# Decode attention over two layers: the last batch's second-layer loads as single parts, four under way

## The chip, the core and the metric

The kernel runs on one core of a Trainium2 chip. The core has a matrix engine (TensorE, rows PE for its matmuls and PEld for its weight loads), VectorE (DVE), ScalarE (ACT), GpSimd (POOL), SyncE (SP, which here only issues transfers), and 16 DMA engines that carry data between HBM and on-chip memory. The metric is the device time of one execution in microseconds (us), lower is better. Times of runs without a profile are given as a median of several; a profiled execution is a single one with its own time.

## The reference

Eight sequences, one new token each, go through two layers with the same weights and the same caches. A layer is attention over a cache of 4096 positions, then a small feed-forward part:

```
x = x + A(layernorm(x))      # attention: 16 query heads, 8 heads of K and V, 256 wide
x = x + B(layernorm(x))      # feed-forward part
x = x + A(layernorm(x))
x = x + B(layernorm(x))
# A: scores = q k^T / 16 ; p = softmax(scores) ; o = p v ; o wo
```

The caches `k_cache` and `v_cache` have the shape (8 batches, 8 heads, 4096 positions, 256) in bfloat16. That is 134 MB each, read from HBM; all else is small. Q has one row per sequence and head, so the work is moving the caches.

## The kernel before, in words

**Units and parts.** The work is a list `units` of 144 entries: (layer, batch, head), or a gap between layers. The second layer of a batch starts while the first layer of the next batch runs. The last section, from index `max(fence)` = 136 on, is the second layer of batch 7, with its heads in the order 2, 3, 6, 7, 4, 5, 0, 1; beside it nothing else is left to do. A head's K and V are each cut into four parts of 512 KB, and a part is moved into one of 31 slots of the tile `slab` (`N_SLOTS`, 4 KB for each of 128 partitions).

**What is done with a part.** A K part is transposed by VectorE into another slot (L605, two instructions). The scores are 16 matmuls for each part (L721, `k_part`). After the four parts of a head come maxima and exponentials (L736 and L755 on VectorE, L745, L773 and L783 on TensorE, L758 and L791 on ScalarE). The V parts follow one head later, 16 matmuls each (L698, `v_part`), and after the fourth `head_out` scales the result (L650). `mark` multiplies with wo (L185). In the first layer, transposed K of six heads and a few parts more stay on the chip for the second layer. So the last section loads 32 parts of V but only 7 of K, for the heads 0 and 1. After the last head comes a last feed-forward part for all batches (L954 to L1035), and the output is stored (L1036).

**The order of loads.** A planner makes the list `loads` before any instruction is written: K parts by the due times `by`, V parts by `plan`. Entries of kind "p" are no transfers: they bring a part that was parked in PSUM back into a slot. `pump()` takes from this list while more than one slot is free (`RESERVE`). It is called whenever a slot is given back: after a V part's matmuls, after the scores of a K part that is needed no more, and after a transpose. All loads go to SP's one queue, in this order, and each waits there until its slot has been read for the last time.

**Pairs.** Where two parts (2j, 2j+1) of the same head are both near in the list and two neighbouring slots are free, `pump` loads both with one transfer of 1 MB. Where no two neighbouring slots are free and at least seven parts are under way, it may put off the load instead (L556). In the last section the trace has 27 loads: 15 of one part (4 of K for head 0, one of K for head 1, 10 of V) and 12 of two (one of K, 11 of V), from 1034.74 to 1076.13 us. A ninth load is held until the one eight before it has landed: the issues at 1047.29 and 1048.53 follow such landings by 0.06 us.

```
            if i % 2 == 0 and two in wide and two in loads[-PAIR_VIEW:]:
                x = take_two() if len(free) > RESERVE + 1 else []
```

Of the kernel before, what the change touches and what calls it, by code (L numbers as in the profile page):

```python
# [25 lines left out]
PAIR_VIEW = 12  # L26
SETTLE = 3
BEFORE = 1


@with_exitstack
def kernel(
# [14 lines left out]
    nc = tc.nc  # L47
# [332 lines left out]
    fence = {}  # L380
# [28 lines left out]
    def fresh(u, s):  # L409

        return u is not GAP and (u[0] == 1 or not stays(u[1], u[2], s))
# [4 lines left out]
    t = 0  # L416
    while t < n_units:
# [5 lines left out]
        n = 1  # L423
# [14 lines left out]
    parts = [(t, s) for t in range(n_units) for s in range(4) if fresh(units[t], s)]  # L438
# [16 lines left out]
    for t in order:  # L455
        for s in range(4):
            i = late_v.get((t, s), 4 * t + s + LAG)
            if t in ends or units[t + 1 : t + 2] == [GAP]:
                i = 4 * t + (6, 6, 7, 7)[s]
            elif t + 2 == n_units:  # L460
                i = 4 * t + (7, 8, 8, 8)[s]
            elif t + 1 == n_units:
                i = 4 * t + (5, 5, 6, 6)[s]
# [3 lines left out]
    loads = []  # L467
    wide = set()
    calm = [any(f < t for f in [-1] + list(fence) if not any(f < e < t for e in ends)) for t in range(n_units + 2)]
    firm = set()  # L470
    at_ease = [all(calm[max(t - SETTLE, 0) : t + BEFORE]) for t in range(n_units + 1)]
    k = 0
    for i in range(4 * n_units + 8):
        n = len(loads)
# [8 lines left out]
        for far in (2, 12):  # L483
            t, q = divmod(i + far, 4)
# [8 lines left out]
    def take():  # L493

        lone = [x for x in free if x ^ 1 not in free]
        x = min(lone or free)
        free.remove(x)
        return x

    def take_two():  # L500

        both = [x for x in free if x % 2 == 0 and x + 1 in free]
        if both:
            free.remove(both[0])
            free.remove(both[0] + 1)
        return both[:1]
# [12 lines left out]
        )  # L519
    extra.append((w4_sb[:], B_w4.rearrange("(c p) d -> p c d", p=128)))  # L520
    n_loads = [0]

    at_out, at_exp, at_max = [], ([], []), ([], [])

    def bring(x, pieces, now):

        dst = slots[x].rearrange("p (e q c x) -> p q c e x", e=4, q=2, c=4)

        def move(q, lo, hi, home):
            src = home.bitcast(BF16).rearrange("p (c e x) -> p c e x", c=4, e=hi - lo)  # L530
            nc.scalar.copy(dst[:, q, :, lo:hi], src)  # L531

        for n, p in enumerate(pieces):
            if now:
                move(*p)
            else:
                (at_out if n < 2 else at_exp[n - 2]).append(lambda p=p: move(*p))

    def pump():
        while loads and len(free) > RESERVE:  # L540
            kind, t, i = loads[-1]
            _, b, g = units[t]
            if kind == "p":
                loads.pop()
                x = take()
                bring(x, park[parked[g, i]], g not in loose)
                kt_of[(1, b, g), i] = x
                continue
            cache, of = (A_k_cache, raw_of) if kind == "k" else (A_v_cache, v_of)
            n, two = 1, (kind, t, i + 1)  # L550
            if i % 2 == 0 and two in wide and two in loads[-PAIR_VIEW:]:
                x = take_two() if len(free) > RESERVE + 1 else []
                if x:
                    n, x = 2, x[0]
                    loads.remove(two)
                elif under_way[0] >= ENOUGH and two in firm:  # L556
                    return
            loads.pop()
            if n == 1:
                x = take()  # L560
            src = cache[b, g].rearrange("(p s e) d -> p s (e d)", s=4, e=8)
            nc.sync.dma_start(
                slab[:, UNIT * x : UNIT * (x + n)].rearrange("p (s d) -> p s d", s=n),
                src[:, i : i + n],
            )
            for m in range(n):
                of[t, i + m] = x + m
            under_way[0] += n
            n_loads[0] += n
            if n_loads[0] >= 8 and extra:  # L570
                nc.sync.dma_start(*extra.pop(0))
# [3 lines left out]
    def let_go(raw):  # L575

        free.append(raw)
        under_way[0] -= 1
        pump()
# [104 lines left out]
    def v_part(t, s):  # L684
        if s == 0:
            n = n_v[0]
            n_v[0] += 1
            at = PO + 4 * (n % n_po)
            pos[t] = pyb[:, at : at + 4].rearrange("p (k h) -> p k h", h=2)
            if n > n_po // 2 and n % (n_po // 2) == n_po // 4:  # L690
                clear.append(PO + 2 * n_po * (1 - n // (n_po // 2) % 2))
            if n % (n_po // 2) == n_po // 2 - 1:
                zero()
        v = v_of.pop((t, s))
        vv = slots[v].rearrange("p (c d) -> p c d", d=Dh)
        for c in range(8):
            for k in range(2):
                nc.tensor.matmul(  # L698
                    pos[t][:, k, :],
                    vv[:, c, k:Dh:2],  # L700
                    pts[t][:, 8 * s + c, :],
                    start=(n_v[0] == 1 and s == 0 and c == 0 and k == 0),
                    stop=True,
                    skip_group_check=True,
                )
        free.append(v)
        under_way[0] -= 1
        pump()

    def k_part(t, s):  # L710
        u = units[t]
        p, b, g = u
        if s == 0:
            assert t not in runs or t in ready
            scs[t] = scb[t % 2][:, 0:64].rearrange("p (c b h) -> p c b h", b=4, h=2)
        key = (u if fresh(u, s) else (1, b, g)), s
        ktv = slots[kt_of[key]].rearrange("p (e c m x) -> p e c m x", e=4, c=2, x=2)
        for c in range(2):
            for db in range(4):
                for x in range(2):  # L720
                    nc.tensor.matmul(  # L721
                        scs[t][:, 2 * s + c, :, :],
                        ktv[:, db, c, :, x],
                        Qblk[run_of[t][0]][:, run_of[t][1], db, x, :, :],
                        start=(db == 0 and x == 0),
                        stop=(db == 3 and x == 1),
                    )
        if p == 2 or not stays(b, g, s) or (g, s) in parked:
            free.append(kt_of.pop(key))
            pump()  # L730
# [154 lines left out]
    for t in range(n_units + 1):  # L885
        cur = t < n_units
        for q in range(4):
            i = 4 * t + q
# [178 lines left out]
```

## Time and profile before

| | |
|---|---|
| median of 3 runs | 1104.24 us (1102.91 to 1107.24) |
| profiled execution | 1111.46 us, span 1109.6 us |
| read from HBM | 443.1 MB, 399 GB/s over the span |
| DMA share, 1041 to 1090 us | 0.98, at 403 GB/s |
| PE busy, 1041 to 1090 us | 34.35 of 49 us |
| DMA share, 1090 to 1110 us | 0.01 |
| landing of the last load of the caches | 1090.54 us |

The page of the profile gives the busy time of each engine, its share in 40 slices of the span, the DMA queues, the chain of waits that ended last, and the costliest groups of instructions. In a group, "out<-in" are the program's names, "x" is the count, and the time in brackets is idle time of the engine and what ended it. "issue" as the end of idle time means that nothing the profile shows ended it. A transfer is listed at SP (SPq) when it is issued; its landing is the update of its semaphore. q1 is the queue of the kernel's transfers; q8 and q14 carry instructions.

### The profile page before, as it was taken

How to read it: one execution, taken by the hardware profiler on the slowest of the kernel's cores; microseconds unless marked ns; L12 is line 12 of the kernel's file. 1: busy time of each engine (PE TensorE's matmuls, PEld its weight loads, DVE VectorE, ACT ScalarE, POOL GpSimd, SP SyncE). 2: the span in 40 equal slices, each digit the busy share in tenths (PEclk: the TensorE clock that was granted, in tenths of full speed). 3: DMA queues.
4: the chain of work that ended last, by engine and by line, in shares of the span. 5: the costliest groups of instructions: out<-in, count | busy, mean ns of one | idle time of the engine just before them, and what ended most of it. 6: DMA issues, size and time to landing. Idle time of an engine off the chain costs nothing.

```text
span 1109.6 us, 46438 instructions
## 1 busy us (share of the span) xinstructions
PE 692.4 (62%) x20757; PEld 647.4 (58%) x20757; DVE 552.8 (50%) x1340; ACT 322.8 (29%) x1409; POOL 104.2 (9%) x156
## 2 busy tenths in 40 slices
PE   3345666667666766657656565766666566666766
PEld 2334666556556655656556565666656565566665
DVE  4447556642664346642566336743466425654222
ACT  1112135221342224221342214321243213421242
POOL 0001011100111001110011001110011100110011
DMA  9999999999999999999999999999999999999992
GB/s 365 403 419 424 402 418 413 426 400 416 420 415 404 404 417 424 425 415 404 419 387 423 405 407 414 405 404 398 417 425 423 405 394 380 413 401 414 416 419 99
DMA packets 92311, 446.10 MB, mean 402 GB/s; under 512 B 9920, under 2 KB 13904, under 8 KB 63440
## 3 DMA queue, kind: packets, MB, share of 16 engines
q1 hardware_dynamic: 92112, 443.14, 98.3%
q8 instruction: 162, 2.65, 0.9%
q14 instruction: 37, 0.30, 0.1%
HBM read 443.10 MB, written 0.01 MB: 399 GB/s over the span
## 4 chain that ended last, share of the span: by engine, by line
DMA 54%; PE 18%; DVE 10%; ACT 10%; issue 6%; SPq 1%; DVEq 0%; ACTq 0%; POOL 0%
DMA slab<-in_A_v_cache_dram 41%; DMA slab<-in_A_k_cache_dram 13%; PE bank L698 6%; DVE slab L605 6%; PE bank L721 4%; ACT pt L791 3%; ACT slab L531 2%; ACT pe L758 2%; DVE small L755 2%; PE bank L745 2%; PE bank L783 1%; ACT pt_far L791 1%; PE bank L773 1%; PE bank L141 1%; PE bank L185 1%
## 5 line engine op out<-in xcount | busy, mean ns | idle before, releaser
L605 DVE STREAM_TRANSPOSE slab<-slab 128x512 f32<-128x512 f32 x626 | 405.1, 686 | 192.0 <-DMA slab<-in_A_k_cache_dram 158.0
L698 PEld LDWEIGHTS <-slab 128*128 128x128 bf16 x8192 | 271.9, 105 | 245.3 <-DMA slab<-in_A_v_cache_dram 180.9
L721 PE MATMUL bank<-Qblk,slab 128*128 128x8 bf16 x8192 | 297.0, 168 | 73.8 <-DVE slab L605 33.8
L698 PE MATMUL bank<-pt,slab 128*128 128x2 bf16 x6336 | 230.7, 166 | 175.1 <-DMA slab<-in_A_v_cache_dram 118.0
L721 PEld LDWEIGHTS <-slab 128*128 128x128 bf16 x8192 | 269.1, 105 | 83.7 <-issue 41.9
L758 ACT ACTIVATE pe<-bank,small 128x32 bf16<-128x32 f32 x256 | 61.4, 297 | 365.9 <-DVE small L755 365.9
L802 POOL TENSOR_TENSOR small<-small 128x2 f32<-128x2 f32 x99 | 69.2, 699 | 706.2 <-DVE small L798 706.2
L755 DVE TENSOR_REDUCE small<-bank 128x2 f32<-128x256 f32 x128 | 54.2, 423 | 101.2 <-PE bank L745 101.1
L791 ACT CAST pt<-bank 32x64 bf16<-32x64 f32 x396 | 80.5, 203 | 81.3 <-PE bank L783 77.8
L698 PE MATMUL bank<-pt_far,slab 128*128 128x2 bf16 x1856 | 65.9, 166 | 42.1 <-DMA slab<-in_A_v_cache_dram 34.1
L798 DVE TENSOR_REDUCE small<-bank 128x2 f32<-128x64 f32 x128 | 27.5, 215 | 111.7 <-ACT pt L791 88.4
L170 ACT CAST Qblk<-bank 32x32 bf16<-32x32 f32 (+1 forms) x292 | 51.5, 176 | 98.5 <-PE bank L164 95.8
L745 PE MATMUL bank<-rows,small 128*128 128x128 bf16 x256 | 48.5, 293 | 30.3 <-DVE small L736 23.4
L783 PEld LDWEIGHTS <-rows 128*128 128x128 bf16 x512 | 33.6, 123 | 47.0 <-issue 46.7
L773 PE MATMUL bank<-pe,small 128*128 128x64 bf16 x128 | 27.2, 213 | 51.8 <-ACT pe L758 46.9
L650 ACT ACTIVATE qT<-bank,small 128x2 bf16<-128x2 f32 x198 | 41.8, 266 | 48.8 <-PE bank L698 46.7
L783 PE MATMUL bank<-pe,rows 128*128 128x64 bf16 x512 | 51.1, 240 | 4.3 <-issue 4.3
L736 DVE TENSOR_REDUCE small<-bank 128x2 bf16<-128x64 f32 x128 | 26.2, 204 | 49.5 <-PE bank L721 48.8
L185 PE MATMUL bank<-qT,wo_sb 128*128 128x1 bf16 (+1 forms) x1152 | 38.7, 165 | 6.7 <-ACT qT L650 5.0
L185 PEld LDWEIGHTS <-wo_sb 128*128 128x128 bf16 x1152 | 35.9, 104 | 7.5 <-issue 6.7
L745 PEld LDWEIGHTS <-small 128*128 128x128 bf16 x256 | 17.4, 106 | 32.6 <-DVE small L736 29.5
L650 ACT ACTIVATE qT<-bank,rz_far 128x2 bf16<-128x2 f32 x58 | 12.2, 265 | 81.8 <-PE bank L698 81.6
(118 smaller groups left out, 448.5 us busy)
## 6 DMA issues: line engine op xcount, KB each, us to landing
slab<-in_A_v_cache_dram SPq DMA_DIRECT2D x270, 512.0 KB, 8.6
slab<-in_A_v_cache_dram SPq DMA_DIRECT2D x121, 1024.0 KB, 12.3
slab<-in_A_k_cache_dram SPq DMA_DIRECT2D x100, 1024.0 KB, 12.0
slab<-in_A_k_cache_dram SPq DMA_DIRECT2D x113, 512.0 KB, 9.3
wo_sb<-in_A_wo_dram SPq DMA_DIRECT2D x4, 896.0 KB, 15.0
wq_sb<-in_A_wq_dram SPq DMA_DIRECT2D x3, 1024.0 KB, 6.8
w_sb<-in_B_w_dram SPq DMA_DIRECT2D x1, 1568.0 KB
w_sb<-in_B_w_dram SPq DMA_DIRECT2D x3, 448.0 KB, 17.0
```

The lines of the kernel that those rows point to most:

```text
L170: nc.scalar.copy(dst, src)
L185: nc.tensor.matmul(y[:, c, :], chunk(wo_sb[:, k, :], c), o[:, k, :], start=first and k == 4 * g and c == 0, stop=True, skip_group_check=True,)
L605: nc.vector.transpose(dst[:, q], src[:, q])
L650: nc.scalar.mul(qT1[:, k : k + 2, b], pos[t][:, :, h], rz_of[t][:, h : h + 1])
L698: nc.tensor.matmul(pos[t][:, k, :], vv[:, c, k:Dh:2], pts[t][:, 8 * s + c, :], start=(n_v[0] == 1 and s == 0 and c == 0 and k == 0), stop= ...
L721: nc.tensor.matmul(scs[t][:, 2 * s + c, :, :], ktv[:, db, c, :, x], Qblk[run_of[t][0]][:, run_of[t][1], db, x, :, :], start=(db == 0 and x ...
L745: nc.tensor.matmul(mzs[t][:, 128 * h : 128 * h + 128], pm[:, h : h + 1].to_broadcast([128, 128]), ident, start=True, stop=True,)
L755: nc.vector.tensor_reduce(nm, mx, AX.X, ALU.max, negate=True)
L758: nc.scalar.activation(pe[:].rearrange("p c b h -> p h (c b)")[:, h], scs[t].rearrange("p c b h -> p h (c b)")[:, h], ACT.Exp, bias=nm[:, ...
L783: nc.tensor.matmul(pp[:, c], sel, pe[:], start=True, stop=True)
L791: nc.scalar.copy(pts[t][sl].rearrange("p (k c) h -> p k c h", c=4), pp[sl, :, :, pb, :].rearrange("p c k h -> p k c h"),)
L802: nc.gpsimd.tensor_tensor(out=rz_of[t], in0=zs, in1=mone, op=ALU.pow)
```

## The change

In the last section (unit index from `final` = 136 on) `pump` no longer makes pairs: every load is one part of 512 KB. Each of these loads also gets a wait: SP issues it only when the load that is four parts ahead in the order of issue has landed. The list `issued` holds a load once for each part that it carries. Earlier loads are as before, but the first four loads of the last section wait for them. The order of the list is the same; without pairs, no part is pulled forward to its neighbour.

```diff
+DEPTH = 4
...
+    issued = []
+    final = max(fence)
...
-            if i % 2 == 0 and two in wide and two in loads[-PAIR_VIEW:]:
+            if t < final and i % 2 == 0 and two in wide and two in loads[-PAIR_VIEW:]:
...
-            nc.sync.dma_start(
+            load = nc.sync.dma_start(
                 slab[:, UNIT * x : UNIT * (x + n)].rearrange("p (s d) -> p s d", s=n),
                 src[:, i : i + n],
             )
+            if t >= final:
+                tc.add_manual_dep(
+                    load.ins,
+                    issued[-DEPTH].ins.name,
+                    mybir.DependencyInfo(mybir.DependencyClass.Sync, mybir.DependencyReason.DATA),
+                    reason="parts under way",
+                )
+            issued.extend([load] * n)
```

## The prediction

> **What bounds the kernel now.** I read the page first. The row of DMA busy tenths is 9 in 39 of 40 slices, so the kernel as a whole streams its caches at what the 16 DMA engines give. The row of q8 holds the fetches of TensorE's instructions: 162 packets with 2.65 MB, that is 16 KB each, for the 41,514 PE and PEld instructions of the page, so one packet for 256 instructions.
>
> ```profile
> span 1109.6 us, 46438 instructions
> ...
> DMA  9999999999999999999999999999999999999992
> ...
> q1 hardware_dynamic: 92112, 443.14, 98.3%
> q8 instruction: 162, 2.65, 0.9%
> ```
>
> The change touches only the last 39 parts, whose first load is issued at 1034.74, so next I read the chain of waits from 1000 us on (columns: start, us, what). Up to 1041 it runs through transfers of V ("DMA slab<-in_A_v_cache_dram", about 8 us each). After that no transfer stands in it: it is TensorE with ScalarE and VectorE between, and pieces called "issue", in which the engine waited for nothing that the profile shows.
>
> ```profile
> 1032.40 8.59 DMA slab<-in_A_v_cache_dram
> ...
> 1048.26 1.13 issue
> ...
> 1053.77 1.55 issue
> ...
> 1066.09 1.11 issue
> ...
> 1089.40 1.70 issue
> ...
> 1095.67 1.86 PE bank L698 x64
> ```
>
> So the last 70 us are bound by TensorE's chain, while the transfers run ahead of it: the last pair lands at 1090.54 and its second part is multiplied at 1096.95. Third, TensorE's timeline. Its "issue" gaps in the tail end at 1043.44, 1049.38, 1055.32, 1061.26, 1067.20, 1073.14, 1079.08, 1085.16 and 1091.10, nearly always 5.94 us and 256 instructions apart. The records of q8 have a packet that starts 2.2 to 2.45 us before each of these ends. I read the gaps as waits for instructions: TensorE used up a block, and the next had not come. They sum to 0.70+1.13+1.55+2.20+1.11+0.85+0.99+0.16+1.70 = 10.4 us.
>
> ```profile
> 1049.38 0.29 PE L721 MATMUL bank<-Qblk,slab 128*128 128x8 bf16 x5 [1.13 <-issue]
> ...
> 1055.32 0.59 PE L721 MATMUL bank<-Qblk,slab 128*128 128x8 bf16 x16 [1.55 <-issue]
> ...
> 1061.26 0.22 PE L721 MATMUL bank<-Qblk,slab 128*128 128x8 bf16 x2 [2.20 <-issue]
> ...
> 1067.20 0.51 PE L698 MATMUL bank<-pt,slab 128*128 128x2 bf16 x13 [1.11 <-issue]
> ```
>
> Last, how long a fetch waits before its packet starts. I take as its request the moment when TensorE enters the block before it, 256 instructions earlier; where TensorE had stalled, that is the end of the stall. From the records, by what SP had issued and had not landed at that moment: nothing outstanding (request at 1091.10, packet at 1092.81) 1.71 us; four parts of 512 KB (requests at 359.26, 365.40 and 948.92) 2.56, 2.25 and 2.31; five parts, median 3.39 of 12; six parts, median 3.64 of 27; eight parts, 3.64 of 28. So the wait grows with the queue up to some five parts and then stays. At four parts the engines were not starved. The window 359 to 362, with three to four parts out and 6.1 us to landing, moved as much as the window 1037 to 1042 with its 9.1 us (418 GB/s):
>
> ```profile
> DMA packets 342, 1.26 MB, mean 421 GB/s; under 512 B 37, under 2 KB 37, under 8 KB 341
> ...
> slab<-in_A_v_cache_dram SPq DMA_DIRECT2D x2, 512.0 KB, 6.1
> ```
>
> **The change part by part.** *The wait.* Each of the 39 parts (7 of K, 32 of V) is issued when the fourth part ahead has landed. Now each is issued earlier than that: the first at 1034.74, where the fourth ahead lands at 1037.24. So every wait binds. Behind a waiting load on SP's queue stand only later loads and the output's store, which starts at 1107.33; POOL issues no transfer. Does a later issue land later? Transfers land in order, 1.24 us apart for single parts. At the landing of part n-4, three parts (3.7 us) lie ahead of part n. A load's own overhead is 0.02 to 0.06 us from the release to the issue, 0.8 to 1.0 us from the issue to the first packet (1107.33 to 1108.12; 1.18 to 2.16 at the start) and 0.35 us from the last packet to the landing (1090.20 to 1090.54): 1.3 us, 2.4 less than the cover. From below it costs nothing. From above: the first 1 MB load of the program, with nearly nothing beside it, took 4.75 us, less 2.43 of transfer 2.3 us, still under 3.7. I take nothing; if the cover goes, the price is that of the third rival.
>
> *Single parts for pairs.* Twelve pairs become 24 loads: 12 more issues of 0.33 us on SP, 0.33 in every 1.25 us, beside SP's waiting. Pairs land 2.43 us apart, singles 1.24, so 0.025 us more a part; over long stretches pairs take 1.23 a part (25 parts, 1059.79 to 1090.54), singles 1.25 (28 parts, 1007.23 to 1042.23) to 1.28 (41 parts, 1007.23 to 1059.79). With 1.265 the last part lands at 1059.79 + 25 x 1.265 = 1091.4 in place of 1090.54, 0.9 us later (ends: 0 and 1.5). The Trainium skill, "DMA: Bandwidth & Descriptors", section "Bandwidth", asks for at least 1 MiB a transfer. By that rule the singles would lose far more; the trace's spacings, with several loads under way, do not show it.
>
> Today this 0.9 us is covered by 1096.95 - 1090.54 = 6.4 us. The order changes too: a pair pulls its second part forward, so the second K part of head 1 (now landing at 1062.2) comes sixth after 1059.79, at 1067.4. VectorE transposes it at 1074.39 (L605), and a reduction of maxima stands behind that; 7 us of margin, 2 if TensorE runs 5 us earlier. Slots do not hold the loads back: from 1044 on some eight are freed in 7 us and five or six are needed.
>
> *The shorter queue.* Four parts are out at any request, so I take a fetch's wait from the nearest row, four parts, median 2.31, against 3.64: 1.33 us less for each of the nine fetches (ends: 0, the row of six parts; 1.9, the row of an empty queue). A stall can give back no more than it has: 0.70+1.13+1.33+1.33+1.11+0.85+0.99+0.16+1.33 = 8.9 us. What is late next is V. Parts now land 3 to 5 us ahead of use in most of the tail, and 2.0 us for the third part of the second head (1056.11 against 1058.07). That spot holds the gain to 2 us until 1058, but 6.3 us of stalls lie behind it. At the end, the last part lands at 1091.4; with 0.04 us to start (as 1039.74 to 1039.78) and 0.59 for its 16 matmuls TensorE is done at 1092.0, where now it is at 1097.5. So the transfers let through 5.5 us at most (6.4 if singles land as pairs do, 4.6 at 1.30 a part). Against 8.9 the cap decides; I take 5.2, as one late landing near the end is enough to lose some tenths. With a fetch's wait cut by only half as much, 0.65 us, the stalls still give 5.4.
>
> The sum: 0 for the waits, the later landings counted in the cap, -5.2. The profiled execution took 1111.46 us (span 1109.6 and 1.9 around it) and would take 1106.3. It lies 7.2 us above the median of the runs shown, 1104.24, for which I forecast 1099.0.
>
> **The rivals.** *The fetch does not follow the depth.* The engines stay full, and what a fetch waits for may be a full engine and not the length of its queue: only three requests fell on four parts, each when SP was late. Then the stalls stay, the later landings stay hidden, and the time is 1104.24, give or take 1: 1105. For it: five and eight parts hardly differ, and at 1085.16 the fetch still waited 3.53 us though no load was issued after 1076.13. Against it: 1.71 us with an empty queue. The Trainium skill, "DMA: Bandwidth & Descriptors", section "Queues, rings and completion order", says that an engine goes round its queues packet by packet; by that rule the depth would not matter, and this rival would hold. The trace's growth from 1.7 to 3.6 us does not settle it.
>
> *Gain kept only in part.* Waits of 3.2 us would cut each stall by 0.4: 3.4 us, 1100.8. This is the slow edge of the forecast and counts with it.
>
> *Slower: the engines run dry.* Place: SP's waits from 1037 on. If a load's overhead is over 3.7 us, part n arrives after part n-1 is through, and each further 0.4 us of overhead adds 0.1 us to each of 38 parts. The first 6.4 us of delay are hidden by the present margin; slower by over 0.5% (5.5 us, about what a measurement here can tell) needs 12 us, 1.58 us a part, an overhead of 5. At 1.6 us a part it gives 1110.5. Against it: the bound of 2.3 us and the 421 GB/s. For it: engines do not finish together (at the end eight stop at 1087.3, the last at 1090.2), so a short queue may idle the quick ones.
>
> That the waits would not take hold is excluded by the issue times above.
>
> **How the numbers follow.** The forecast has 0.65, the fetch that does not follow the depth 0.25, the dry engines 0.10. The forecast's own range is 1097 (cap of 6.4 and scatter of the runs) to 1102. The bound for faster, 1098.7, lies just beyond its centre: I give 0.31 of its 0.65 to faster, the rest to no change, together with the first rival. The range from 1096.5 to 1105.7 takes in both and leaves out the third.
>
> **What would show it.** Right: SP issues 0.1 us after a landing, four parts apart, and loads land some 5 to 6 us after issue; parts still land 1.24 to 1.28 apart and the last at 1091; the ends of TensorE's "issue" gaps come nearer than 5.94 us, and the gaps sum to under 4 us; waits for V appear after 1045; L954, now at 1098.54, starts near 1093.3. Wrong: gaps of the same 10 us, or DMA tenths under 9 in the tail with landings over 1.4 us apart.

## The result, and the profile after

The changed kernel takes 1109.41 us (median of 8 runs, 1108.62 to 1113.84) against 1105.02 us of the kernel before (8 runs): a ratio of 1.0041, with a 95% interval of 1.0029 to 1.0054. It is slower by about 4.5 us. I had forecast 1099.0 us and a range up to 1105.7, and had given the dry engines, the rival that came nearest, a chance of 0.10. The profiled execution took 1113.84 us, span 1112.0.

The page of the changed kernel still shows full DMA tenths, but its row of GB/s falls in two slices near the end:

```profile
span 1112.0 us, 46468 instructions
...
DMA  9999999999999999999999999999999999999994
GB/s 351 396 419 423 403 397 424 424 400 415 419 412 421 409 416 423 424 400 403 420 390 424 414 411 415 411 393 416 418 424 425 412 407 393 417 409 417 361 326 164
...
q8 instruction: 162, 2.65, 0.9%
```

Slices 38 and 39 move 361 and 326 GB/s, and the last one 164 where the kernel before had 99: the stream of V reaches further towards the end. A tenth counts an engine as busy while a packet of its is open, and in this tail one 4 KB packet in 19 is open for 0.26 us or more, in place of the usual 0.159 (they are counted with the last streaming kernel below). So the tenths stay at 9 and the GB/s tell the loss. The transfers from 1041 to 1088 us, first of the kernel before, then of the changed one:

```profile
DMA packets 3626, 19.47 MB, mean 414 GB/s; under 512 B 405, under 2 KB 405, under 8 KB 2111
...
slab<-in_A_v_cache_dram SPq DMA_DIRECT2D x11, 1024.0 KB, 11.5
```
```profile
DMA packets 4357, 15.96 MB, mean 340 GB/s; under 512 B 486, under 2 KB 486, under 8 KB 4347
```

In the same 47 us the changed kernel moves 15.96 MB in place of 19.47. From its landings, the first of the 39 parts arrives at 1039.86 and the last at 1099.38, so 38 parts take 59.5 us, 1.566 each; before it was 1042.23 to 1090.54, 1.271 each. Of the signs that I had named for being wrong, landings over 1.4 us apart came, and the tenths of the page did not fall. The chain of waits of the changed kernel (start, us, what), which had no transfer behind 1041 before, now runs through loads of V to the end, each issued when an earlier one has landed:

```profile
1046.82 0.56 PE bank L732 x16
...
1060.32 5.86 DMA slab<-in_A_v_cache_dram
...
1080.12 6.44 DMA slab<-in_A_v_cache_dram
...
1092.35 7.03 DMA slab<-in_A_v_cache_dram
1099.38 0.05 issue
1099.42 0.60 PE bank L709 x16
```

TensorE's waits (us in total, times, longest) show what took the place of what, first those of the kernel before, from 1041 to 1092 us, then those of the changed one, from 1041 to 1101:

```profile
PE bank L721 <- issue: 7.3, 5, 2.2
PE bank L698 <- issue: 2.3, 3, 1.1
...
PE bank L185 <- issue: 0.9, 1, 0.9
PE bank L698 <- DMA slab<-in_A_v_cache_dram: 0.7, 1, 0.7
```
```profile
PE bank L709 <- DMA slab<-in_A_v_cache_dram: 6.7, 8, 1.5
PE bank L732 <- issue: 5.0, 3, 2.2
PE bank L186 <- issue: 2.2, 2, 1.6
...
PE bank L709 <- issue: 0.5, 1, 0.5
```

The "issue" gaps are 7.7 us in place of 10.5, and the waits for V are 6.7 us in place of 0.7 (L709 is L698 of before, L732 is L721, L186 is L185). Counted from the same instruction of TensorE (1362 matmuls before the last one), the kernel before needs 64.76 us to its last matmul and the changed one 70.01: 5.25 us more, all in the section that was changed.

### The profile page after: what moved, and what is told of

Same layout as the page of the kernel before. It is cut to its first block, busy times and chain, and to the rows that moved or that the text cites. A ratio compares the mean times of both kernels' runs of the same rounds, so it can differ in the third digit from the quotient of the medians.

```text
span 1112.0 us, 46468 instructions
## 1 busy us (share of the span) xinstructions
PE 694.0 (62%) x20757; PEld 648.2 (58%) x20757; DVE 552.5 (50%) x1340; ACT 322.8 (29%) x1409; POOL 104.5 (9%) x156
## 4 chain that ended last, share of the span: by engine, by line
DMA 57%; PE 17%; DVE 10%; ACT 9%; issue 6%; SPq 1%; DVEq 0%; ACTq 0%; POOL 0%
DMA slab<-in_A_v_cache_dram 43%; DMA slab<-in_A_k_cache_dram 14%; DVE slab L616 6%; PE bank L709 6%; PE bank L732 4%; ACT pt L802 3%; ACT pe L769 2%; ACT slab L534 2%; DVE small L766 2%; PE bank L756 1%; PE bank L794 1%; ACT pt_far L802 1%; PE bank L142 1%; PE bank L784 1%; DVE park L622 1%
## 5 line engine op out<-in xcount | busy, mean ns | idle before, releaser
L709 PEld LDWEIGHTS <-slab 128*128 128x128 bf16 x8192 | 272.2, 105 | 250.6 <-DMA slab<-in_A_v_cache_dram 189.0
L709 PE MATMUL bank<-pt,slab 128*128 128x2 bf16 x6336 | 231.2, 166 | 179.7 <-DMA slab<-in_A_v_cache_dram 123.7
L732 PE MATMUL bank<-Qblk,slab 128*128 128x8 bf16 x8192 | 297.1, 168 | 71.1 <-DVE slab L616 34.9
L732 PEld LDWEIGHTS <-slab 128*128 128x128 bf16 x8192 | 269.3, 105 | 79.6 <-DVE slab L616 41.2
L709 PE MATMUL bank<-pt_far,slab 128*128 128x2 bf16 x1856 | 65.7, 166 | 42.3 <-DMA slab<-in_A_v_cache_dram 35.2
L186 PE MATMUL bank<-qT,wo_sb 128*128 128x1 bf16 (+1 forms) x1152 | 38.8, 165 | 8.0 <-ACT qT L661 5.0
L186 PEld LDWEIGHTS <-wo_sb 128*128 128x128 bf16 x1152 | 36.0, 104 | 8.9 <-issue 8.1
```

The costliest lines, as they stand in the source:

```text
L186: nc.tensor.matmul(y[:, c, :], chunk(wo_sb[:, k, :], c), o[:, k, :], start=first and k == 4 * g and c == 0, stop=True, skip_group_check=True,)
L709: nc.tensor.matmul(pos[t][:, k, :], vv[:, c, k:Dh:2], pts[t][:, 8 * s + c, :], start=(n_v[0] == 1 and s == 0 and c == 0 and k == 0), stop= ...
L732: nc.tensor.matmul(scs[t][:, 2 * s + c, :, :], ktv[:, db, c, :, x], Qblk[run_of[t][0]][:, run_of[t][1], db, x, :, :], start=(db == 0 and x ...
```

## The experiments

**What is in the change: single parts, or the wait?** First the single parts alone, without the wait:

```diff
-            if t >= final:
-                tc.add_manual_dep(load.ins, issued[-DEPTH].ins.name, ...)
```

> The changed kernel without its wait: single parts in the last section, at most eight under way. If the wait is what costs (theories 'fetch' and 'overhead'): within 0.15% of the kernel before, last landing near 1091.5. If single parts or their order cost (theory 'singles'): about as slow as the changed kernel, +0.4%, with the last landing near 1099.

Measured: 0.9999 of the kernel before (0.9987 to 1.0011), last landing 1088.28, 1.287 us a part. Then the wait with the pairs kept:

```diff
-            if t < final and i % 2 == 0 and two in wide and two in loads[-PAIR_VIEW:]:
+            if i % 2 == 0 and two in wide and two in loads[-PAIR_VIEW:]:
```

> The changed kernel's wait with the pairs of the kernel before: a pair also waits for the fourth part ahead, so up to five parts are out. If the wait is what costs: slower than before, but by less than the changed kernel, +0.1 to +0.3%, with parts about 1.4 us apart. Theory 'singles': as the kernel before.

Measured: 1.0048 (1.0035 to 1.0060), as slow as the changed kernel, so the size I expected was too small. TensorE's waits from 1041 to 1092 us in this kernel:

```profile
PE bank L709 <- DMA slab<-in_A_v_cache_dram: 10.6, 8, 2.5
```

Single parts and their order cost nothing that these runs can tell; the loss is the wait's. Up to five parts out as pairs are no better than four singles: for most of this stretch only two or three loads are then under way.

**Where the depth begins to cost.** The changed kernel with another `DEPTH`:

```diff
-DEPTH = 4
+DEPTH = 6    # and 5, and 3
```

> The changed kernel with DEPTH 6. Theory 'fetch': six parts cover 7.7 us and a delay of 1 to 2 us fits in, so parts land 1.27 to 1.32 apart, the last one near 1090, and the time is within 0.15% of the kernel before. If the waits on landings cost by themselves, however many parts are out: +0.2% or more.

> The changed kernel with DEPTH 5: between four and six. Theory 'fetch': about 1.35 us a part, 3 to 5 us later than before at the last landing, which the 6 us of margin at the end hide nearly: 0 to +0.2%.

> The changed kernel with DEPTH 3, the suspected cost made larger. Quiet, three parts gave 1.76 us a part; with fetches 1.9 to 2.1. 38 parts at 2.0 end about 16 us after the changed kernel's last landing, and as that kernel has no margin left, the time rises by the same: +1.6 to +2.0% over the kernel before. If its tail is bound elsewhere (TensorE's chain, order of loads), it rises by less than 1%.

| DEPTH | ratio to the kernel before | 95% interval | us a part |
|---|---|---|---|
| 3 | 1.0140 | 1.0116 to 1.0165 | 1.803 |
| 4 (the change) | 1.0041 | 1.0029 to 1.0054 | 1.566 |
| 5 | 0.9976 | 0.9965 to 0.9988 | 1.341 (1.281 in the second run) |
| 6 | 1.0006 | 0.9995 to 1.0017 | 1.289 |

Depth 3 lost a little less than the 1.6 to 2.0% that I had expected. There TensorE's waits from 1041 to 1095 us are nearly all for V, and those for instructions are gone:

```profile
PE bank L709 <- DMA slab<-in_A_v_cache_dram: 17.2, 14, 2.9
...
PE bank L732 <- issue: 0.7, 1, 0.7
```

So waiting on a landing costs nothing by itself (depth 6), and from 5 to 4 the stream breaks. Depth 5 beats both kernels, which none of my theories had said. I ran it again:

> DEPTH 5 once more, with more rounds: the first time it took 0.9976 of the kernel before (0.9965 to 0.9988). If that is the depth's doing (a fetch starts a few tenths sooner, 5.70 us apart in the streaming kernel against 6.14 at depth 8, over nine fetches 2 to 4 us): 0.997 to 0.999 again. If it was chance: 1.000.

Measured: 0.9975 (0.9962 to 0.9989), 1103.86 us against 1105.91, so it holds.

**Is it the fetches?** My first theory for the loss was that a fetch of TensorE's instructions holds one DMA engine, and that with four parts out everything waits for that engine. Several kernels were made to test it. The first only streams, at seven depths, with TensorE idle and then busy:

```
for busy in (False, True):
    if busy: 5600 matmuls of 128x2, from the end of the quiet half on
    for depth in (1, 2, 3, 4, 5, 6, 8):
        32 loads of 512 KB, each waiting for the one `depth` before it
```

> A kernel that only streams: 32 parts of 512 KB (4 KB a partition) at each depth of 1, 2, 3, 4, 5, 6 and 8 parts under way, first with TensorE idle, then again while TensorE runs 5600 small matmuls, so that its instructions are fetched all the time. All of the model's computation is left out and the output is a copy of an input. Theory 'fetch' (the changed kernel lost 1.57 - 1.25 us a part because a fetch holds one of the 16 engines for about 1 us, and with four parts out every later issue waits for that engine): quiet half at depth 4 about 1.25 to 1.30 us a part, busy half at depth 4 about 1.5, and the difference between the halves shrinks to under 0.1 at depth 8. Theory 'overhead' (four parts do not cover a load's own delay, with or without fetches): depth 4 is about 1.55 in both halves, and the quiet half reaches 1.25 only at depth 5 or 6.

Quiet, a part took 3.83, 2.33, 1.76, 1.28, 1.28, 1.28 and 1.28 us at the seven depths (in the middle of each stage, between its 10th and 31st landing). TensorE's matmuls ended at 611 us, during depth 2, so the busy half told nothing on depth 4 with fetches. It gave a second stage of depth 4 without them, which again took 1.28 us a part, here from 694 to 734 us:

```profile
DMA packets 4355, 15.83 MB, mean 396 GB/s; under 512 B 492, under 2 KB 492, under 8 KB 4354
```

The quiet half told one thing that my prediction had needed, a load with nothing beside it (20 to 120 us, the last figure is us from issue to landing):

```profile
slab<-in_A_k_cache_dram SPq DMA_DIRECT2D x26, 512.0 KB, 3.8
```

It takes 3.81 us, 2.53 more than the 1.28 that a part takes in a full stream. By its packets, 0.96 us go by from the issue to the first packet, 2.56 from there to the end of the last one, and 0.30 more to the landing. So the two ends make up half of the 2.53; the other half is that the packets of a load alone are spread over 2.56 us in place of 1.28: some 17 of the 128 take 0.26 us or more, 0.54 on average, where the usual packet takes 0.159. Then the same with TensorE busy throughout (15000 matmuls, the busy half alone):

> The streaming kernel again (the model's computation is left out), now with TensorE running 15000 small matmuls beside all seven depths, since its 5600 ended before depth 4 was reached. Quiet, the first run gave 3.83, 2.33, 1.76, 1.28, 1.28, 1.28, 1.28 us a part at depths 1, 2, 3, 4, 5, 6, 8, and 3.81 us for a load alone: four parts cover 5.12 us, 1.3 more than that. Theory 'fetch': a fetch of about 1 us on one engine eats that margin, so depth 4 goes to 1.45 to 1.6 with a fetch each 5 to 6 us, depth 5 to about 1.35, depth 8 stays under 1.32. Theory 'overhead': depth 4 stays at 1.28, and the changed kernel's 1.57 is from something else than fetches. For the fetch itself: if its wait follows the depth (my prediction), fetches are about 4.6 us apart at depth 4 and 5.9 at 8; if not (my first rival), 5.5 or more at both.

| depth | 1 | 2 | 3 | 4 | 5 | 6 | 8 | none |
|---|---|---|---|---|---|---|---|---|
| us a part | 3.84 | 2.36 | 1.94 | 1.59 | 1.31 | 1.27 | 1.30 | |
| us between fetches | 3.84 | 4.56 | 5.10 | 5.86 | 5.70 | 6.21 | 6.14 | 3.7 |

From depth 4 on a stage holds only five to eight fetches, so the second row is good to a few tenths. The stages of depth 4 (270 to 307 us) and 5 (320 to 354 us), by their transfers:

```profile
DMA packets 3510, 12.85 MB, mean 347 GB/s; under 512 B 390, under 2 KB 390, under 8 KB 3504
...
q8 instruction: 6, 0.10, 1.0%
```
```profile
DMA packets 3741, 13.70 MB, mean 403 GB/s; under 512 B 414, under 2 KB 414, under 8 KB 3735
...
q8 instruction: 6, 0.10, 1.1%
```

This looked like the theory's proof, with 1.59 as in the changed kernel. The kernel itself with few fetches said otherwise:

```diff
-        for c in range(8):
+        for c in range(8 if t < final else 1):
...
-            for db in range(4):
+            for db in range(4 if t < final else 1):
```

> The changed kernel with 2 of 16 matmuls left in each score and each V part of the last section (the output is then not the model's), so that TensorE's instructions in the tail, and with them its fetches from 1041 us on, fall from ten to about four. Theory 'fetch': parts then land about 1.35 us apart and the last one near 1091 (1039.9 + 38 x 1.35). Theory 'overhead': still 1.55 us apart, last landing near 1099.

Measured: 1.429 us a part, last landing 1092.09, so between the two theories. With 4 fetches in place of 10 the excess over 1.28 fell from 10.9 to 5.7 us, and three of the late landings had no fetch near them. So I varied the rate of fetches alone:

```
STAGES = ((0, 0), (512, 330), (256, 650), (128, 1300), (2, 1600))   # columns, matmuls
for each stage: the matmuls, beside 48 loads at depth 4
```

> The streaming kernel at depth 4 throughout (the model's computation is left out), five stages of 48 parts, with TensorE idle and then running matmuls of 512, 256, 128 and 2 columns, so that a block of 256 instructions lasts about 28, 14, 7 and 5.9 us. Theory 'fetch': the time above 1.28 us a part grows with the number of fetches in a stage, by about 1.4 us a fetch (in the run before, 1.59 - 1.28 = 0.31 us a part with a fetch in 5.86 us, 3.7 parts: 1.1; in the changed kernel 38 x 0.286 over 10 fetches: 1.1; take 1.1 to 1.6): about 1.28, 1.34, 1.41, 1.55, 1.6 us a part. If TensorE's work as such (its reads of on-chip memory) slows the transfers, the stage of 512 columns is slow too, 1.5 or more.

Measured: 1.408, 1.479, 1.473, 1.514 and 1.533 us a part with 0, 2, 4, 9 and 11 fetches. With no fetch at all depth 4 already lost 0.13 us a part, where the first streaming kernel had lost nothing, so fetches were not the sole cause here. Nor does TensorE's work as such show: counted over whole stages, the one with 512 columns took 1.463 us a part and the one with none 1.478. The last kernel has no TensorE work, and disturbs the stream with copies of 16 KB on one engine:

```
STAGES = ((4, 0), (4, 0), (4, 64), (4, 16), (5, 0), (5, 16), (8, 0), (8, 16))   # depth, a copy every so many parts
for each stage: 64 loads at that depth; nc.scalar.dma_start(16 KB, one engine) at part 8 of every so many
```

> The streaming kernel without TensorE, so without any fetch (the model's computation is left out): stages of 64 parts at depths 4, 4, 4, 4, 5, 5, 8, 8. In the third stage one extra copy of 16 KB by a single DMA engine is issued from ScalarE's queue at part 8; in the fourth, sixth and eighth such a copy at every 16th part. What is to be explained: depth 4 without fetches took 1.28 us a part in one stage and 1.41 in another that began at the program's start. Theory 'restart': four parts leave about 1.3 us to spare; an engine that once runs out pays about a microsecond for its next packet, so any disturbance (a fetch, a cold start) begets further ones. Then: first stage 1.35 to 1.45, second 1.28, third over 1.35 for many parts after its one copy, fourth 1.45 or more, depth 5 at most 1.30 quiet and 1.35 disturbed, depth 8 under 1.31 in both. Theory 'fetch' alone: first and second 1.28, third 1.30 (one loss of 1 to 1.5 us), fourth 1.36 to 1.40.

| stage | 4 | 4 | 4, one copy | 4, four copies | 5 | 5, four copies | 8 | 8, four copies |
|---|---|---|---|---|---|---|---|---|
| us a part | 1.462 | 1.465 | 1.485 | 1.408 | 1.279 | 1.313 | 1.279 | 1.299 |
| packets of 0.26 us or more | 349 | 342 | 381 | 366 | 1 | 33 | 1 | 0 |

The first stage (20 to 90 us, depth 4) and the fifth (400 to 460 us, depth 5), by their transfers, with no other work on the core:

```profile
DMA packets 6876, 25.04 MB, mean 358 GB/s; under 512 B 763, under 2 KB 763, under 8 KB 6876
...
q1 hardware_dynamic: 6876, 25.04, 98.7%
```
```profile
DMA packets 6758, 24.62 MB, mean 410 GB/s; under 512 B 749, under 2 KB 749, under 8 KB 6758
...
q1 hardware_dynamic: 6758, 24.62, 102.8%
```

Neither theory had expected the second stage, and theory 'restart' had expected 1.45 or more in the fourth. In this kernel and the one before it, four parts under way lose 0.13 to 0.19 us a part with nothing beside them, whether started cold or after a pause. The first streaming kernel held 1.28 in both of its stages. It ran on another chip than these two, and no streaming kernel ran on two chips, so a difference between chips is not ruled out. It would not be the whole answer: on the same chip as the first streaming kernel, the changed kernel with few matmuls lost 0.15 us a part, with three late landings away from any fetch. Copies add nothing steady at depth 4; at 5 and 8 four of them cost 0.3 to 0.5 us each, where a copy's packet takes about 0.62 us. A packet of 4 KB takes 0.159 us. At depth 4 one in 20 of some 7000 takes 0.26 us or more, about a quarter of these 0.6 and over; at depth 5, one packet in 6920. In the changed kernel it is 261 of 4921 between 1036 and 1096 us, at depth 6 of the same kernel 41 of 4757. I read these as packets of engines that had run dry and were waiting for data of the next load, as a load alone shows them. That reading is not tested further.

One more thing can be read from the landings. The landing of a load is counted by 16 updates of its semaphore, as many as there are DMA engines. Between the first and the last of them lie 1.0 and 1.2 us on average in the two depth 4 stages that ran clean, 1.6 to 1.8 in the three that lost with nothing beside them, and 1.2 in the quiet stage of depth 5. Four parts leave 4 x 1.28 - 3.81 = 1.3 us to spare, so by stage the loss goes with a spread above that. By single loads it hardly does: in those three stages a landing came over 1.4 us after the one before it in 39 of 119 cases in which the load four ahead had been spread over more than 1.31 us, and in 8 of 33 in which it had not. So the spread can be the loss's cause or its effect, and why a stage of depth 4 can also run clean stays open.

**Spending the margin at the end.** Depth 5, and 3 for the last eight parts:

```diff
-                    issued[-DEPTH].ins.name,
+                    issued[-DEPTH if len(loads) >= 8 else -3].ins.name,
```

> DEPTH 5, and 3 for the last eight parts. There the transfers run 5 to 7 us ahead of TensorE; at depth 3 a part takes 1.94 us in the streaming kernel in place of 1.31, so the last lands about 5 us later and uses that margin up, while fetches come 5.1 us apart in place of 5.7. With two fetches in that stretch the gain is at most 1.2 us and the loss up to 2: between 0.997 and 1.002 of the kernel before, and not clearly better than DEPTH 5 alone.

Measured: 0.9992 (0.9977 to 1.0007), as expected and not better than depth 5 alone: its profile has a new wait of 1.0 us for the last V part.

## Why the prediction was wrong, point by point

*What bounds the tail* stands. The "issue" gaps are waits for instructions: the streaming kernel, whose TensorE does nothing but matmuls, fetches every 3.7 us with no load outstanding and every 6.1 to 6.2 with six or eight. In the kernel before they came every 5.94 us.

*"I take nothing" for the wait* is the step that failed, and it decided the result. I had added up a load's overhead from two ends, 0.95 us to the first packet and 0.35 behind the last, to 1.3 us. I called the program's first load with its 2.3 us a bound from above. A load alone shows 2.53 us, so the sum was half of the truth and the "bound" lay under it. The ends were right (0.96 and 0.30 us); the half left out is that the packets of a load alone are spread over 2.56 us. Even so four parts (5.12 us) should cover 3.81, and yet held at four the stream took 1.566 us a part, where six took 1.289. What the sum by one stream left out, as I read it, is that a load lands when the slowest of 16 engines has landed it, so the others wait behind a window that only that one opens. That the wait at depth 4 costs the time is shown; this mechanism for it is argued. I had named the uneven engines in the third rival ("a short queue may idle the quick ones") and gave them no price of their own. The window from 359 to 362 us, in which I saw four parts move 421 GB/s, was a queue passing through four parts for a moment. It was no stream held at four.

*The third rival's price* was right. "At 1.6 us a part it gives 1110.5"; measured were 1.566 and 1109.41. Its condition, an overhead of 5 us, was wrong: the stream breaks with one of 2.53.

*The shorter queue* failed too. "A fetch's wait from the nearest row, four parts, median 2.31" came from three requests at which SP was late and the queue was emptying. Held at four parts the ten fetches of the changed kernel's tail waited 2.3 to 5.5 us, median 3.7, where before it was 3.65. In the streaming kernel they come 5.86 us apart at depth 4, against 6.14 at 8. So the first rival, which I gave 0.25, was right on the fetch, and it was hidden by the third. The Trainium skill, "DMA: Bandwidth & Descriptors", section "Queues, rings and completion order", had an engine go round its queues packet by packet, so that the depth would not matter. From four parts up the runs nearly agree (5.7 to 6.2 us between fetches); from none to three they do not (3.7 to 5.1).

*Single parts for pairs* stands: 0.9999 with the singles alone, and the 0.9 us that I put on the last landing was hidden. The Trainium skill, "DMA: Bandwidth & Descriptors", section "Bandwidth", asks for at least 1 MiB a transfer; with six loads of 512 KB under way these runs lose nothing.

*The cap by the last landing* was the right way to count, with the wrong landing: TensorE ended 0.64 us behind the last part, as I had it, but that part came at 1099.38 in place of 1091.4.

## What to carry to other kernels

A row in which a queue happens to be short is no evidence for a queue that is held short; the depth that a stream needs is found by holding it there. A stream of loads alone does that, but not in one run: the first one said that four were enough, the next two that they were not. If a window on landings is opened by the slowest engine, as I read it, it wants more than a load's own time divided by its share of the bandwidth: here 3.81 / 1.28 gives three parts, at four a part took up to a quarter longer, and five were enough or nearly so (1.28 to 1.34 us a part). Where a limit is worth trying, its neighbours are too: 4 lost 0.4%, 5 gained 0.25%.

## What the runs showed of the hardware that I had not expected

Five parts under way stream at 1.279 us a part with an idle TensorE, exactly as eight do; four took 1.41 to 1.47 in three such stages and 1.28 in two others, of a kernel on another chip. The busy share of the DMA engines hardly tells four from five (98.7% against 102.8% of 16 engines), the GB/s do (358 and 410).

Depth 5 is faster than the kernel before by 0.25% in two sets of runs (0.9976 and 0.9975), and depth 6 is not. From the same instruction of TensorE to its last matmul the two profiles show 63.71 and 63.40 us against 64.76, so 1.05 and 1.36 less. Most of that is in the waits for instructions, here those of the second profile, from 1036 to 1099 us:

```profile
PE bank L732 <- issue: 6.6, 4, 2.2
...
PE bank L186 <- issue: 1.5, 1, 1.5
...
PE bank L709 <- issue: 1.3, 3, 0.7
```

They sum to 9.4 us, and to 9.7 in the first profile, against 10.5 before and 10.7 at depth 6. The fetches' waits in the tail have the same median (3.64 and 3.65 us, 3.65 before), but the same eight of them sum to 28.1 and 28.5 us, against 29.3 before and 29.0 at depth 6. So a little of the gain that I had forecast at four parts seems to come at five. These are single profiles, and what shortens a few of the fetches is open.
